# A planned attention and gated-MLP kernel: copies as 64-bit additions on GpSimd, more exponentials on VectorE, and a new order of work

## The chip, the cores and the metric

The kernel runs on one core of one Trainium2 chip. The core has five engines with an instruction queue each: TensorE (PE, matrix multiplication into the accumulation memory PSUM), VectorE (DVE), ScalarE (ACT, functions such as the exponential), GpSimd (POOL) and SyncE (SP, which here only issues transfers). The metric is the time of one execution on the device in microseconds (us); the median of several runs is given.

## What is computed

All tensors are bfloat16. Attention A and a gated MLP B read the same tokens x (B's own input is not used), and a gate per token mixes them:

```python
S, D, H, F = 2048, 512, 32, 1376           # Dh = D // H = 16
q, k, v = split(x @ wqkv)                   # 32 heads of 16
p = softmax(einsum("hqd,hkd->hqk", q, k) * Dh ** -0.5)
a = merge(einsum("hqk,hkd->hqd", p, v)) @ wo
b = ((x @ w_gate) * (x @ w_up)) @ w_down
g = sigmoid((x * gate_w).sum(-1, keepdims=True))
return g * a + (1 - g) * b
```

The exponentials of the scores, 32 x 2048 x 2048 of them, are most of the work outside PE.

## The kernel before

**A plan written by the program.** Nothing here is scheduled on the chip. When the program is built, the class `_Sched` plays the five engines forward in time with a table of durations. At every step each free engine takes a job by rules that read parameters from `PAR`; most of these are lists of (count, value), one value for each slot of 4 us of planned time (`g`). Each job taken becomes an instruction at the end of its engine's queue, and `_Plan.emit` adds the semaphore waits that its inputs and its reused buffers need. So the lists in `PAR` set the order of the work, and each engine then runs its queue strictly in that order.

**PE in halves.** Nearly all matmuls use half of the array's rows (64) and a quarter of its columns (32 or 17). `pe64` (line 1620) issues four of them, one for each column tile: a unit. The plan keeps two streams of units, r = 0 and r = 1, for the two halves of the rows.

**Scores.** Queries are taken in 32 groups ("quads") of four heads by 512 queries, keys in 16 tiles of 128: 512 key steps. A key step has four cells; a cell is one unit of score matmuls into one PSUM bank, 128 keys x 512 queries for one head. Seven of the eight banks are shared by the cells and the other results (`bank_pick`, `bank_put`); the eighth collects the weighted values.

**Two ways to the exponential.** A key step is of kind A or D.
- Kind A goes to ACT (`try_act`, `exp`, line 1718). One instruction takes one bank, or two adjacent ones.
- Kind D goes to DVE (`dve_pass`, `dpass`, line 1754): a scaled score plus a constant, cut at zero and written as a 16-bit integer, is the bit pattern of a bfloat16 that approximates the exponential. To make it accurate, four variants are summed: the pattern itself (v = 0) and three copies with 32 v added to each 16-bit integer (`copy`), each multiplied by values scaled by 2^(−v/4) (`Vs`, line 1777). A copy covers a whole key step, 128 x 2048 integers ("full"), or half of one. It is made on DVE (`copy_dve`, line 1760) or on POOL (`try_pool`, line 1764), where it is a 32-bit addition of two tensors, the pattern and the broadcast constant `cadd`. `dlst` holds the six key tiles that may be of kind D (`dks`), and `dl` caps how many of them a quad takes. Patterns lie in the buffers `DB` and, late in the run, in the space of `wv` and `wk`.

**Values.** `v_job` multiplies the cells by V with a column of ones: 8 matmuls for a key step of kind A, 4 x 8 for one of kind D. After 16 key steps DVE empties the bank (`o_copy`, line 1830); the denominators go by SP's transfers through DRAM and come back as the broadcast tile `rb`, and POOL multiplies (`mult`, line 1923, as a `ptask` of the plan).

**Fill units.** Between these run the projections, the MLP and the output matmuls (`fill`), a list of units in the order of their due times; each is emptied by DVE. `xt` units turn a tile of x by a multiplication with the identity `ident`, in 32 x 64 pieces in this kernel.

**DVE against POOL.** The plan keeps POOL's work and DVE's copies apart in time (`dve4_until`, `lock_v`), and each POOL copy and `mult` waits for the last DVE copy planned before it (`last4`).

**The beginning.** `prologue` loads x and the first weights, makes `ident` on POOL (line 1947), clears `QM`, turns the first 512 tokens and projects the first heads.

Of the kernel before, what the change touches and what calls it, by code (L numbers as in the profile page):

```python
# [10 lines left out]
I32 = mybir.dt.int32  # L11
# [121 lines left out]
class _Step:  # L133
    __slots__ = ("q", "kt", "kind", "cells", "nexp", "eops", "nv", "vleft", "buf", "npass", "ncp", "cpb", "okt", "cptodo", "ydone", "refs", "half", "acc")


class _Sched:
# [39 lines left out]
    def g(self, name):  # L177
        v = self.tab[name]
        return v[min(int(self.now / 4.0), len(v) - 1)]
# [38 lines left out]
    def next_d(self):  # L218
        while self.qd < self.NG:
# [7 lines left out]
            if self.dlst[m] and self.nd[m] < lim:  # L227
# [16 lines left out]
                e.acc = self.nd[m] <= self.g("acc")  # L244
                if e.acc:
                    e.cpb[3] = e.buf
                    e.cptodo = e.cptodo[:4]
# [17 lines left out]
    def bank_pick(self, kind, r):  # L265
# [15 lines left out]
        if kind == "D" and self.g("dpair"):  # L281
            a = self.dmate
            if a is not None and a[0] != r:
                self.dmate = None
                if a[1] in fr:
                    return a[1]
            d = 1 - 2 * r
            for b in fr:
                if b + d in fr and (b - d not in fr or self.g("dpair") > 1):
                    self.dmate = (r, b + d)  # L290
                    return b
# [71 lines left out]
    def v_job(self, r):  # L363
# [16 lines left out]
        if self.owner == 1 - r and self.g("hold") > 0 and not self.g("ph"):  # L380
            o = sum(1 for x in self.vq[1 - r] if x[0] <= self.now + 1e-9 and x[1].q == oq)
            if o and n < o + self.g("hold"):
                return False
# [122 lines left out]
    def y_unref(self, e, op):  # L506
        e.refs += 1
        e.eops.append(op)
        if e.acc and e.refs == 5:
            self.accq.append((e, list(e.eops), self.now + self.par["adel"]))  # L510
            self.at(self.now + self.par["adel"])
        elif e.refs == 7:
            self.dlast[e.buf] = list(e.eops)
            self.dfree.append(e.buf)
# [84 lines left out]
    def f_start(self, r):  # L599
# [13 lines left out]
        u.bank = self.bank_get("F")  # L613
        u.half = r
        self.fact.append(u)
        self.f_slice(u, r)
        return True

# [7 lines left out]
    def try_pe(self, r):  # L626
        if self.hf[r] > self.now + 1e-9:
            return False
        if self.g("ph"):
            if self.pe_phase(r):  # L630
                return True
            if r == 0 and self.par["t0"] <= self.now < self.par["warmto"] and self.owner is None and self.oq == 0:
                if self.hw:
                    self.o_evop = self.hw.warm_mm(r)
                self.log("pe%d" % r, 0.216, ("W", r))
                self.take(r, 0.216)
                return True
            return False
        if self.aout < self.g("alook") and self.s_a(r):
            return True  # L640
        if self.dout < self.g("dlook") and self.s_d(r):
            return True
        prog = (sum(self.apos) + sum(self.dpos)) / 64.0
        debt = self.target(prog) - self.fdone
        prio = self.g("prio") if debt <= self.g("fdebt") else self.g("prio2")
        for ch in prio:
            if ch == "A":
                if self.s_a(r):
                    return True
            elif ch == "D":  # L650
                if self.dout < self.g("dlook2") and self.s_d(r):
                    return True
            elif ch == "V":
                if self.v_job(r):
                    return True
            elif ch == "C":
                if self.f_cont(r):
                    return True
            elif ch == "S":
                if debt >= -self.g("flead") and self.f_start(r):  # L660
                    return True
        return False

    def pe_phase(self, r):
        self.tick[0] += 1
        o = self.ov[0].get(self.tick[0], 0)
        if o == 6:
            return False
        if o and (self.s_a, self.s_d, self.v_job, self.f_cont, self.f_start)[o - 1](r):
            return True  # L670
# [48 lines left out]

    def try_act(self):  # L720
# [15 lines left out]
        self.tick[2] += 1  # L736
        o = self.ov[2].get(self.tick[2], 0)
# [10 lines left out]
        if grp is not None and self.cfree[grp]:  # L748
            n = 1
            if len(self.cfree[grp]) > 1:  # L750
                for i in range(len(rd)):
                    j = next((j for j in range(i + 1, len(rd)) if abs(rd[j][4] - rd[i][4]) == 1), None)
                    if j is not None and (i == 0 or self.g("apick")):
                        x, y = rd[i], rd[j]
                        rd.remove(x)
                        rd.remove(y)
                        rd[:0] = [x, y]
                        n = 2
                        break
                if n == 1 and o == 2:  # L760
                    n = 0
                if n == 1 and o != 1 and any(abs(x[4] - rd[0][4]) == 1 and x[0] <= self.now + self.g("await") for x in self.aready):
# [6 lines left out]
        cells = [self.cfree[grp].pop(0) for _ in range(n)]  # L769
        cells.sort()  # L770
        rd.sort(key=lambda x: x[4])
        dur = 0.833e-3 * 512 * n + 0.051
# [10 lines left out]
        t = self.now + dur + 0.12 + 0.05  # L783
# [20 lines left out]
    def try_dve(self):  # L804
# [3 lines left out]
        self.tick[1] += 1  # L808
        o = self.ov[1].get(self.tick[1], 0)
        if o == 4:  # L810
            return False
        if o == 1 and self.lock_v <= now and self.copy_dve():
            return True
        if o == 2 and self.dve_pass(now):
            return True
        if o == 3 and self.dve_evac(now):
            return True
# [1418 lines left out]
```

## Time and profile before

| | |
|---|---|
| three runs, median (lowest to highest) | 714.14 us (712.85 to 715.62) |
| span of the profiled execution | 713.9 us |
| granted TensorE clock, mean | 0.995 |
| matmuls | 22279 |
| DVE, ACT, POOL instructions | 1095, 888, 426 |

Times in the views are microseconds unless marked ns. A row of a group names line, engine and operation, output <- input by the program's names, the shapes and the count, then the busy time in total and the mean of one instruction, then the idle time before them and what ended it. PEld is PE's weight load, which overlaps matmuls. The end of a matmul is modelled, and successive instructions of an engine overlap in the records, so that the mean of one instruction is longer than the distance from its start to the next one's start.

### The profile page before, as it was taken

Reading aid. Unit: us, or ns where it says so; the run is one execution under the profiler, and the core shown is the slowest. Engines: PE = TensorE matmul, PEld = TensorE weight load, DVE = VectorE, ACT = ScalarE, POOL = GpSimd, SP = SyncE. Lnnn points to the kernel's source line nnn. Section 1 sums busy time; section 2 is a strip of 40 time slices with the busy share of each in tenths; the row PEclk is TensorE's granted clock in tenths of the full one; section 3 lists DMA queues with packets and bytes.
Section 4 is the critical chain, followed back from the end, with each engine's and each line's share of the span. In section 5 each row is a group of like instructions: output and inputs, shape, how many; then the busy total and the mean of one; then the engine's idle time right before and its main releaser. Section 6 shows DMA issues by size and latency. Waiting matters only on the chain.

```text
span 713.9 us, 48146 instructions
## 1 busy us (share of the span) xinstructions
PE 697.6 (98%) x22279; PEld 370.7 (52%) x22279; DVE 659.7 (92%) x1095; ACT 686.5 (96%) x888; POOL 443.4 (62%) x426
## 2 busy tenths in 40 slices
PE   7999999999999999999999999999999999999997
PEld 4555455555544545555554455545454555555453
DVE  4898999999999999999999999999999999999994
ACT  5799999999999999999999999999999999999995
POOL 3374686786655555666675666777675647777631
PEclk8999999999999999999999999999999999999999
DMA  9101422103010100100001010100001010010100
GB/s 189 35 5 31 113 66 57 13 4 108 12 41 5 35 20 15 32 12 28 12 18 29 13 34 20 35 12 14 26 6 42 11 40 16 12 28 17 31 19 33
DMA packets 32121, 22.98 MB, mean 32 GB/s; under 512 B 17356, under 2 KB 28524, under 8 KB 31920
## 3 DMA queue, kind: packets, MB, share of 16 engines
q1 hardware_dynamic: 30784, 18.86, 10.7%
q8 instruction: 174, 2.85, 1.7%
q0 software_dynamic: 176, 0.53, 0.3%
q10 hardware_dynamic: 960, 0.52, 0.3%
q14 instruction: 27, 0.22, 0.1%
HBM read 12.23 MB, written 2.36 MB: 20 GB/s over the span
## 4 chain that ended last, share of the span: by engine, by line
PE 84%; DVE 7%; ACT 5%; issue 2%; DMA 1%; POOL 0%; SPq 0%; ACTq 0%; DVEq 0%
PE ps L1620 84%; DVE DB L1754 3%; ACT PT L1718 2%; ACT xT L1718 1%; DVE DB L1760 1%; DMA wg<-in_B_w_gate_dram 1%; DMA DB<-in_A_x_dram 1%; ACT wd L1718 1%; ACT hT L1718 0%; DVE wk L1754 0%; DVE oc L1830 0%; DVE wv L1760 0%; DVE hT L1806 0%; DVE oraw L1830 0%; ACT wu L1718 0%
## 5 line engine op out<-in xcount | busy, mean ns | idle before, releaser
L1620 PE MATMUL ps<-QM,KT 64*32 64x512 bf16 x8192 | 515.6, 380 | 4.6 <-ACT PT L1718 1.4
L1718 ACT ACTIVATE PT<-ps 128x1024 bf16<-128x1024 f32 (+1 forms) x453 | 384.7, 972 | 4.4 <-PE ps L1620 3.4
L1764 POOL TENSOR_TENSOR DB<-DB,cadd 128x512 int32<-128x512 int32 (+1 forms) x249 | 264.0, 1085 | 141.0 <-DVE DB L1760 88.4
L1754 DVE TENSOR_SCALAR DB<-ps 128x512 int16<-128x512 f32 x501 | 330.2, 687 | 22.6 <-PE ps L1620 18.6
L1620 PE MATMUL ps<-DB,Vs 64*17 64x512 bf16 x2912 | 267.7, 376 | 1.4 <-issue 0.3
L1620 PEld LDWEIGHTS ps<-QM,KT 64*32 64x32 bf16 x8192 | 161.1, 90 | 169.4 <-ACT PT L1718 49.0
L1718 ACT ACTIVATE xT<-ps 128x1024 bf16<-128x1024 f32 (+1 forms) x279 | 237.1, 951 | 1.7 <-PE ps L1620 1.3
L1620 PE MATMUL ps<-PT,Vp 64*17 64x512 bf16 x1556 | 219.4, 376 | 0.2
L1620 PE MATMUL ps<-xT,Vp 64*17 64x512 bf16 x936 | 151.9, 377 | 0.5 <-DVE oraw L1830 0.4
L1620 PE MATMUL ps<-xT,wu 64*32 64x512 bf16 x1376 | 113.7, 377 | 0.0
L1620 PE MATMUL ps<-xT,wg 64*32 64x512 bf16 x1376 | 113.0, 377 | 0.5 <-issue 0.4
L1760 DVE TENSOR_SCALAR DB<-DB 128x2048 int16<-128x2048 int16 (+1 forms) x170 | 109.8, 676 | 1.6 <-PE ps L1620 1.3
L1620 PE MATMUL ps<-DB,Vp 64*17 64x512 bf16 x1008 | 99.9, 377 | 0.7 <-DVE oc L1830 0.2
L1620 PE MATMUL ps<-wd,hT 64*32 64x512 bf16 x1408 | 100.2, 377 | 0.0
L1620 PEld LDWEIGHTS ps<-DB,Vs 64*17 64x17 bf16 x2912 | 73.4, 86 | 34.5 <-PE ps L1620 9.2
L1620 PEld LDWEIGHTS ps<-PT,Vp 64*17 64x17 bf16 x1556 | 55.5, 86 | 16.6 <-PE ps L1620 5.7
L1718 ACT ACTIVATE wd<-ps 128x1024 bf16<-128x1024 f32 (+1 forms) x74 | 61.4, 948 | 0.3 <-PE ps L1620 0.2
L1764 POOL TENSOR_TENSOR wv<-DB,cadd 128x512 int32<-128x512 int32 (+1 forms) x41 | 44.6, 1102 | 22.2 <-DVE DB L1760 12.7
L1764 POOL TENSOR_TENSOR wk<-DB,cadd 128x512 int32<-128x512 int32 (+1 forms) x33 | 35.5, 1092 | 21.0 <-DVE DB L1760 10.7
L1764 POOL TENSOR_TENSOR DB<-wk,cadd 128x512 int32<-128x512 int32 (+1 forms) x32 | 35.0, 1120 | 16.4 <-DVE DB L1760 12.4
L1620 PEld LDWEIGHTS ps<-xT,wu 64*32 64x32 bf16 x1376 | 36.3, 91 | 15.5 <-DVE DB L1754 2.5
L1620 PEld LDWEIGHTS ps<-xT,Vp 64*17 64x17 bf16 x936 | 38.2, 87 | 11.7 <-PE ps L1620 1.4
(111 smaller groups left out, 890.9 us busy)
## 6 DMA issues: line engine op xcount, KB each, us to landing
rb<-rscr SPq DMA_DIRECT2D x16, 256.0 KB
QM<-qraw SPq DMA_DIRECT2D x124, 16.0 KB, 2.2
oc<-oraw SPq DMA_DIRECT2D x60, 32.0 KB, 2.3
out_dram<-ost SPq DMA_DIRECT2D x12, 128.0 KB, 1.8
wd<-in_B_w_down_dram SPq DMA_DIRECT2D x10, 128.0 KB, 2.5
wu<-in_B_w_up_dram SPq DMA_DIRECT2D x12, 96.0 KB, 3.3
wg<-in_B_w_gate_dram SPq DMA_DIRECT2D x12, 96.0 KB, 2.2
OT<-in_A_x_dram SPq DMA_DIRECT2D x2, 256.0 KB, 4.6
```

What stands on the lines that cost most here:

```text
L1620: o = pe.matmul(dst, lhs, rhs, start=st, stop=sp, tile_position=(64 * r, 32 * cc), skip_group_check=True)
L1718: return self.P.op("act", lambda a: a.activation(dst, src, ACT.Exp, scale=self.ES), deps)
L1754: return self.dve(lambda v: v.tensor_scalar(dst, src, self.YB, 0.0, ALU.add, ALU.max), deps)
L1760: return self.dve(lambda e: e.tensor_scalar(o, a, 32.0 * v, None, ALU.add), deps)
L1764: lambda e: e.tensor_tensor(o.bitcast(I32), a.bitcast(I32), self.cadd[:, v, :].bitcast(I32).to_broadcast([128, n]), ALU.add),
```

## The change

The result stays the same formula; who does what, and when, changes.
- **Copies on POOL** become one 64-bit integer addition with a constant in the instruction: 32 v in each of the four 16-bit lanes. `cadd` goes. The planned durations are 1.026 (full) and 0.595 (half) in place of 1.849 and 0.997. A dummy addition in the prologue calls the operation once.
- **More kind D**: the lists give 178 of 512 key steps to DVE's way (150 before).
- **`mult`** moves from POOL to DVE, and so does one addition of the tail.
- **Exponentials** may take three banks of equal spacing (`tri`, `evenly`). **Evictions of kind D** may pair any two cells whose banks are adjacent, of two key steps too.
- **`xt` units** become four full-array matmuls that occupy both halves (`x_full`, `x_turn`).
- **The identity** is made on DVE: a counter along the row, its transpose, and a comparison.
- **`q_mask`** waits for the clearing of its own half of `QM` only.
- Branches that were switched off (`acc`, `ov`, `warm_mm`, another PE policy) are deleted.
- **All lists of `PAR` are new.** They come from a beam search over the plan. They change the order on every engine, and how many copies DVE makes.

Instructions in the two built programs, where they differ in number:

| | before | after |
|---|---|---|
| ACT exponentials of one, two, three banks | 302, 573, 0 | 719, 307, 1 |
| DVE evictions of kind D, one and two banks | 592, 4 | 700, 6 |
| DVE copies, full and half | 233, 21 | 27, 1 |
| POOL copies, full and half | 21, 371 | 410, 193 |
| `mult` on POOL, on DVE | 16, 0 | 0, 16 |
| weighted-value matmuls | 7696 | 8368 |
| matmuls that turn x in `xt` units | 128 | 16 |

```diff
     def copy(self, eng, src, dst, v, hs, deps):
...
-            lambda e: e.tensor_tensor(o.bitcast(I32), a.bitcast(I32), self.cadd[:, v, :].bitcast(I32).to_broadcast([128, n]), ALU.add),
-            deps + [self.r["cadd"]],
+        return self.P.op("pool", lambda e: e.int64_add(o.bitcast(I64), a.bitcast(I64), 32 * v * 0x0001000100010001), deps)
...
             if both and bl >= self.g("gfull"):
-                hs, dur = [0, 1], 1.849
+                hs, dur = [0, 1], 1.026
             elif bl >= self.g("ghalf"):
-                hs, dur = [h], 0.997
+                hs, dur = [h], 0.595
...
     def mult(self, bi, deps):
-        return self.P.op("pool", lambda g: g.tensor_tensor(self.OT[:, bi % 8, :], self.oc[:], self.rb[:], ALU.mult), deps)
+        return self.dve(lambda v: v.tensor_tensor(self.OT[:, bi % 8, :], self.oc[:], self.rb[:], ALU.mult), deps)
...
+    def x_turn(self, bank, ch, t, deps):
...
+            for kt in range(4):
+                c0 = 128 * kt
+                o = pe.matmul(self.ps[:, bank, c0 : c0 + 128], x[:, c0 : c0 + 128], self.ident[:], start=True, stop=True, skip_group_check=True)
...
     def exp(self, banks, cells, deps):
-        if len(banks) == 2:
-            s = cells[1][1] - i
-            dst = t[:, i : cells[1][1] + 1 : s, :]
-            src = self.ps[:, banks[0] : banks[1] + 1, :]
+        if len(banks) > 1:
+            dst = t[:, i : cells[-1][1] + 1 : cells[1][1] - i, :]
+            src = self.ps[:, banks[0] : banks[-1] + 1, :]
...
     def dve_pass(self, now):
-                if y[2] is x[2] and abs(y[4] - x[4]) == 1 and (y[4] - x[4]) * (y[3] - x[3]) > 0:
+                if abs(y[4] - x[4]) == 1 and (y[2] is x[2] or max(x[2].buf, y[2].buf) < self.par["ND"]):
...
+    def identity(self):
+        a, b = self.io[:, 0, :], self.io[:, 1, :]
...
+        for k in range(5):
+            w = a.rearrange("p (x y z) -> p x y z", y=2, z=1 << k)[:, :, 1, :]
+            o = dve(lambda v, w=w, k=k: v.tensor_scalar(w, w, float(1 << k), None, ALU.add), [o])
+        o = dve(lambda v: v.transpose(b, a), [o])
+            r.append(dve(lambda v, lo=lo, hi=hi: v.tensor_tensor(self.ident[lo:hi, lo:hi], self.io[lo:hi, 0, :], self.io[lo:hi, 1, :], ALU.is_equal), [o, z]))
...
-        i0 = pool(lambda g: g.memset(self.ident[:], 1.0))
-        i1 = pool(lambda g: g.affine_select(self.ident[:], self.ident[:], [[-1, 128]], ALU.is_equal, 0.0, base=0, channel_multiplier=1), [i0])
+        i1 = self.identity()
...
+        l0 = pool(lambda g: g.memset(self.lib[:], 0.0))
+        pool(lambda g: g.int64_add(self.lib[:].bitcast(I64), self.lib[:].bitcast(I64), 0), [l0])
...
- 'dl': ((2, 6), (1, 4), (4, 3), (1, 4), (3, 2), (4, 3), (2, 4), (3, 5), (3, 4), (3, 5), (6, 6), (4, 5),
+ 'dl': ((7, 6), (1, 5), (2, 6), (4, 5), (19, 6), (1, 3), (5, 6), (2, 5), (17, 6), (3, 5), (5, 7), (15, 6), (2, 7), (1, 6), (4, 7), (8, 6), (1, 7),
...
```

439 lines of the change are left out of this document (184 added, 255 removed), and 37 rows, old and new, of the table PAR.

## The prediction

> **What bounds the kernel now.** I read the page first: its span, the busy time of the engines and the shares of the chain that ended last.
>
> ```profile
> span 713.9 us, 48146 instructions
> PE 697.6 (98%) x22279; PEld 370.7 (52%) x22279; DVE 659.7 (92%) x1095; ACT 686.5 (96%) x888; POOL 443.4 (62%) x426
> PE 84%; DVE 7%; ACT 5%; issue 2%; DMA 1%; POOL 0%; SPq 0%; ACTq 0%; DVEq 0%
> ```
>
> One number looks decisive and is not: the 98% of PE (TensorE). A matmul row lasts about 376 ns while its successor starts earlier, and the chain gives PE 84% because some matmul is always under way. So I take a price per unit of work for each engine from the timeline, where a group and the next one show the start-to-start spacing, and multiply by counts. ScalarE (ACT) first: six two-bank exponentials and the row after them, then four one-bank ones and the row after them.
>
> ```profile
> 303.21 5.64 ACT L1718 ACTIVATE PT<-ps 128x1024 bf16<-128x1024 f32 x6
> 308.64 2.04 ACT L1718 ACTIVATE xT<-ps 128x1024 bf16<-128x1024 f32 x2
> 21.50 2.06 ACT L1718 ACTIVATE wg<-ps 128x512 bf16<-128x512 f32 x4 [4.35 <-PE ps L1620]
> 23.43 2.21 ACT L1718 ACTIVATE wu<-ps 128x512 bf16<-128x512 f32 x4
> ```
>
> (308.64 − 303.21) / 6 = 0.905 us for a pair, (23.43 − 21.50) / 4 = 0.4825 us for a single: 0.4225 us for each cell and 0.06 us for each instruction. A cell is one bank, 128 keys by 512 queries; there are 2048. VectorE (DVE) and PE in the same view:
>
> ```profile
> 310.81 1.87 DVE L1754 TENSOR_SCALAR DB<-ps 128x512 int16<-128x512 f32 x3
> 312.61 0.68 DVE L1760 TENSOR_SCALAR DB<-DB 128x2048 int16<-128x2048 int16 x1
> 313.21 0.68 DVE L1760 TENSOR_SCALAR wk<-DB 128x2048 int16<-128x2048 int16 x1
> ...
> 438.77 0.10 PEld L1620 LDWEIGHTS ps<-wd,hT 64*32 64x32 bf16 x4
> 438.81 0.10 PEld L1620 LDWEIGHTS ps<-PT,Vp 64*17 64x17 bf16 x4
> 438.99 0.10 PEld L1620 LDWEIGHTS ps<-QM,KT 64*32 64x32 bf16 x4
> 439.02 0.10 PEld L1620 LDWEIGHTS ps<-DB,Vs 64*17 64x17 bf16 x4
> ```
>
> A one-bank DVE eviction costs (312.61 − 310.81) / 3 = 0.60 us, and a full DVE copy (four cells) 313.21 − 312.61 = 0.60 us as well. On PE two streams of weight loads interleave, one for each half of the array; in each a unit of four matmuls follows the last after 0.21 to 0.22 us. I take 0.216 us for half the array, so 0.108 us of PE for a unit.
>
> Counts are from the two built programs' instruction lists. Before: 596 evictions (592 singles, 4 pairs) take 600 cells, so ACT has 1448 cells in 875 exponentials, 573 pairs and 302 singles.
> - ACT: 573 x 0.905 + 302 x 0.4825 + about 6 for the rest = 670 us.
> - PE: 5532 units x 0.108 = 597 us, and 2 us of transposes.
> - DVE: 592 x 0.60 + 4 x 1.13 + 233 full copies x 0.60 + 21 half copies x 0.335 = 506 us, and some 130 us of other evictions and small work: about 636 us.
> - GpSimd (POOL): 443 us busy by the page.
>
> How full the engines are by stretch (busy us, then counts in brackets):
>
> ```profile
> 0.00:20.00 20.00, 16.25 (x319) 9.69 (x327) 9.72 (x22) 10.08 (x17) 7.60 (x17) 0.85 0.96 189
> 20.00:100.00 80.00, 79.03 (x2588) 43.21 (x2580) 72.82 (x130) 76.51 (x116) 47.97 (x45) 1.00 0.17 41
> 300.00:400.00 100.00, 99.13 (x3160) 52.26 (x3151) 95.77 (x158) 99.45 (x111) 63.91 (x63) 1.00 0.07 18
> 400.00:500.00 100.00, 99.37 (x3296) 51.92 (x3288) 94.68 (x155) 99.88 (x125) 70.57 (x71) 1.00 0.08 22
> 700.00:714.00 14.00, 9.42 (x286) 4.31 (x269) 5.19 (x12) 5.59 (x9) 2.24 (x2) 0.98 0.12 41
> sum 714.00, PE 697.61 PEld 370.69 DVE 659.70 ACT 686.49 POOL 443.36; mean PE 69.76 PEld 37.07 DVE 65.97 ACT 68.65 POOL 44.34
> ```
>
> From 300 to 500 ACT is idle for 0.67 of 200 us; DVE lacks 9.6 us. PE's 3296 matmuls from 400 to 500 are 824 units, 89 of 100 us. ACT is the engine whose work lies nearest the span: ACT bounds the middle, with PE and DVE close behind. The 44 us between 713.9 and 670 I split: idle at the ends 9.9 (0 to 20) + 3.5 (20 to 100) + 8.4 (700 to 714) = 21.8; other idle 27.5 − 21.8 = 5.7; and 686.5 − 670 = 16.5 inside "busy" rows that lasted longer than their work. So 22 us of waiting lie inside the run. Who waits for whom:
>
> ```profile
> PEld ps L1620 <- ACT PT L1718: 50.4, 197, 0.9
> PEld ps L1620 <- ACT xT L1718: 28.1, 109, 0.6
> PEld ps L1620 <- DVE DB L1754: 27.5, 120, 1.5
> POOL DB L1764 <- DVE DB L1760: 115.4, 59, 10.0
> ```
>
> PE's weight loads wait for ACT and DVE to give banks back (50.4, 28.1, 27.5 us), and POOL stands 115.4 us behind DVE's copies.
>
> **The change, part by part.** First, *112 cells move from ACT to DVE* (178 key steps instead of 150: 712 cells). After the change ACT has 1336 cells in 1027 exponentials: 719 singles, 307 pairs, one triple. ACT: 719 x 0.4825 + 307 x 0.905 + 1.3 + 6 = 632 us, 38 less; 47 saved by the cells, 9 given back by 152 more instructions. The triple has no row; between a pair (0.905) and three singles (1.45) it is one instruction, so the choice is worth nothing.
>
> Second, *the copies go to POOL*. These rows give the prices (mean ns of one in the last column but one):
>
> ```profile
> L1754 DVE TENSOR_SCALAR DB<-ps 128x512 int16<-128x512 f32 x498 | 326.8, 684 | 21.9 <-PE ps L1620 18.0
> L1754 DVE TENSOR_SCALAR DB<-ps 128x1024 int16<-128x1024 f32 x3 | 3.7, 1222 | 0.7 <-PE ps L1620 0.7
> L1760 DVE TENSOR_SCALAR DB<-DB 128x2048 int16<-128x2048 int16 x160 | 106.5, 692 | 1.6 <-PE ps L1620 1.3
> L1760 DVE TENSOR_SCALAR DB<-DB 128x1024 int16<-128x1024 int16 x10 | 4.2, 418 | 0.0
> L1764 POOL TENSOR_TENSOR DB<-DB,cadd 128x512 int32<-128x512 int32 x236 | 239.9, 1040 | 133.0 <-DVE DB L1760 82.2 <-PE ps L1620 33.7 <-DVE wk L1760 6.9
> L1764 POOL TENSOR_TENSOR DB<-DB,cadd 128x1024 int32<-128x1024 int32 x13 | 24.5, 1893 | 8.1 <-DVE DB L1760 6.1 <-PE ps L1620 2.0
> L1923 POOL TENSOR_TENSOR OT<-oc,rb 128x512 bf16<-128x512 f32 x16 | 20.5, 1281 | 33.0 <-DVE DB L1760 26.0 <-DVE wv L1760 5.4 <-DVE wk L1760 1.6
> L1956 POOL MEMSET Vp<- 128x1024 bf16 x1 | 1.0, 1013 | 0.0
> L1957 POOL MEMSET erow<- 128x512 f32 x1 | 0.5, 529 | 0.0
> ```
>
> DVE loses 206 full copies (−123.6) and 20 half ones (418 ns, of which I count 0.335 as in the 0.08 us overlap of the others: −6.7). It gains 108 single evictions (+64.8), two pairs (+2.3 at 1.13, the 1222 ns row less overlap) and 16 multiplications of 128x512 (+9.6). Sum −53.6: about 582 us.
>
> POOL gets 410 full and 193 half copies as 64-bit additions with one tensor input. No row shows that operation. From above: the 32-bit additions with two inputs, 1893 and 1040 ns for the same bytes (1.67 ns per 32-bit word). From below: 64-bit elements each at the memset's step, (1013 − 529) / 512 = 0.945 ns, 512 elements, about 0.53 for a full copy. Nearest I think is the memset at one 32-bit word per step: one stream, 1013 ns full and 529 ns half. That value gives 410 x 1.013 + 193 x 0.529 = 517 us; the upper bound 410 x 1.893 + 193 x 1.040 = 977 us. Only the second end touches the forecast (rival 1).
>
> [...] No run here yet shows the one-input form.
>
> Third, *what the move adds to PE*. A key step on DVE needs 4 variants x 8 value matmuls instead of 8: 28 x 24 = 672 matmuls, 168 units, +18.1 us. PE: 597 + 18 + 2 = 617 us. The transposes of x shrink from 128 small matmuls to 16 full ones that take both halves; both forms are near 2 us in the first 20 us, where the engines wait for data: nothing.
>
> Fourth, *the rest*. The identity on DVE is a dozen tiny operations ahead of the first transposes; DVE stands idle there until 4.93 us. [...]
>
> ```profile
> 4.93 0.69 DVE L2009 CAST xT<-ps 128x512 bf16<-128x512 f32 x1 [3.27 <-PE ps L2002]
> 18.93 2.04 POOL L1764 TENSOR_TENSOR DB<-DB,cadd 128x512 int32<-128x512 int32 x2 [9.96 <-DVE DB L1760]
> ```
>
> [...] The 16 multiplications now wait on DVE for a broadcast DMA, and evictions queue behind them, for whose banks PE waits: 0 to 1 us each, 0 to 16 us; I take 0 and keep 16 for the range, since between the DMA and the use the plan keeps the same margin as before. The new order of work takes no work away; it can only shift the 22 us of waiting.
>
> **The sum.** ACT stays the longest: 632, against PE 617, DVE 582, POOL 517. Add the ends, 21.8, since no edit shortens the loads or the tail: 654. Then the inner waiting, 22 us before. Less: 206 copies of 0.60 us no longer stand ahead of evictions on DVE, and POOL's 115 us behind them go. More: PE would fill 617 of some 640 us instead of 599 of 692 us, so a lost slot is harder to win back. Bounds: none (654) to nearly double (694). I take a third, 7 us: 632 + 22 + 7 = 661 us. The trace's span of 713.9 us is the median of 714.14 us to 0.03%, so nothing is added around it: 661 us.
>
> **The rivals.**
> 1. *POOL's price.* If the 64-bit addition costs what the 32-bit ones did, POOL needs 977 us, and with its first copy at 18.9 us the run ends near 1000 us: slower. It decides from the price at which POOL reaches about 625 us (661 less its start and the tail): with a half at 0.52 of a full, 625 / (410 + 193 x 0.52) = 1.22 us for a full copy; at 1.33 us the time is back at 714. For it: the bytes and the engine are the same. Against: the memset rows, and one input instead of two.
> 2. *PE's slots are the bound already.* If PE cannot fill more than the 599 / 713.9 = 84% of now, 617 / 0.84 = 735 us: slower. For it: the chain is 84% PE, and weight loads wait for banks. Against: 89% in the stretch 400 to 500, and ACT busy for 99.7% of 300 to 500. [...]
> 3. *Singles starve ACT.* Here eight singles took (444.74 − 439.58) / 8 = 0.645 us each:
>
> ```profile
> 439.58 5.37 ACT L1718 ACTIVATE PT<-ps 128x512 bf16<-128x512 f32 x8
> 444.74 1.61 ACT L1718 ACTIVATE xT<-ps 128x1024 bf16<-128x1024 f32 x2
> ```
>
>    Twice as many singles may mean more of this. If the waiting inside the run grows with their number, 22 x 719 / 302 = 52 us in place of 7: 632 + 22 + 52 = 706; half of that growth gives 691 us. Against: the four singles above ran at 0.4825.
> 4. *The ends shrink too.* ACT is idle for 13.4 us before 100 us; if the new order halves that and the inner waiting vanishes, 632 + 15 = 647 us.
>
> **How the numbers follow.** Forecast 58%, rival 4 15%, rival 3 18%, rival 1 5%, rival 2 4%. The range 644 to 694 takes in rival 4 and the cheaper half of rival 3, and leaves out the two slow rivals and rival 3's worst. About 0.5% (3.6 us) is what this measurement can tell from no change. Faster: 58 + 15 + 18 = 91%; within 0.5%: 1%, from prices of POOL between; slower: 8%.
>
> **What would show it right or wrong.** POOL: full copies near 1.0 us start to start, 500 to 550 us busy; above 1.2 us the forecast falls. ACT: about 1040 instructions and 632 us of work, over 98% busy in the middle. DVE: near 590 us busy, with few copy rows. PE: 5700 units in some 640 us are 890 in 100 us of the middle (7120 matmuls in 200 us); if it stays near 824 while ACT shows gaps, rival 2 holds. If ACT's singles average well over 0.60 us and PE's weight loads wait more than 106 us on banks, rival 3. A multiplication on DVE with an idle stretch before it would show the added wait.

## The result, and the profile after

The changed kernel takes 702.29 us in the median of 4 runs (699.92 to 705.51), beside 713.65 us before: ratio 0.9844 (95% interval 0.9812 to 0.9877). It is faster, by 1.6%, where 7.4% were forecast, and outside the range of 644 to 694 us. The profiled execution has a span of 703.7 us and its own time of 705.51 us. The same kernel was measured twice more, on other chips, as the base of experiments. One run of after_again and two of after_third are over 1.5% slower than the fastest beside them; without these the medians are 686.9 and 688.9 us.

| chip | before, median | changed, median (lowest to highest) | ratio (95%) | fetch of a program packet, median |
|---|---|---|---|---|
| first | 713.65 | 702.29 (699.92 to 705.51) | 0.9844 (0.9812 to 0.9877) | 1.10 us |
| of after_again | 710.70 | 687.29 (680.95 to 692.84) | 0.9640 (0.9593 to 0.9687) | 0.96 us |
| of after_third | 711.39 | 690.58 (684.22 to 696.21) | 0.9732 (0.9694 to 0.9770) | 0.96 us |

The kernel before moves by 3 us from chip to chip, the changed one by 15, and by up to 12 on one chip. On the two later chips the time lies inside the forecast range, but 26 and 30 us above the 661 that were forecast. The last column is how long one transfer of TensorE's instruction queue (q8 in the page), a packet of 16.4 KB of its program, took in the profiled execution; it is read from the trace's transfer records.

The page of the changed kernel, first chip: span, busy times, that queue (packets, MB, share of 16 engines' span), and the chain that ended last:

```profile
span 703.7 us, 49393 instructions
PE 682.0 (97%) x22839; PEld 393.0 (56%) x22839; DVE 624.5 (89%) x1008; ACT 660.0 (94%) x1040; POOL 545.3 (77%) x617
...
q8 instruction: 178, 2.92, 1.8%
...
PE 92%; DVE 4%; issue 2%; POOL 1%; ACT 0%; DVEq 0%; POOLq 0%; ACTq 0%
```

POOL's 545 us and ACT's 1040 instructions are what was forecast. DVE is busy for 624.5 us where near 590 were foretold. ACT is busy for 94% only, and the chain is PE for 92% (84% before). By stretch; the columns are the stretch, its length, the busy us and counts of PE, PEld, DVE, ACT and POOL, then the granted clock, the share of the transfer engines and GB/s:

```profile
200.00:300.00 100.00, 99.24 (x3408) 58.62 (x3402) 87.95 (x138) 98.07 (x160) 89.96 (x110) 1.00 0.10 26
300.00:400.00 100.00, 96.29 (x3264) 53.22 (x3256) 92.57 (x141) 94.17 (x143) 85.70 (x90) 0.98 0.07 18
400.00:500.00 100.00, 97.17 (x3340) 56.24 (x3320) 88.72 (x141) 94.88 (x158) 80.37 (x94) 1.00 0.09 25
```

The first of these stretches in the kernel before (the prediction shows the other two):

```profile
200.00:300.00 100.00, 98.80 (x3033) 49.92 (x3025) 96.79 (x161) 98.37 (x124) 54.29 (x51) 1.00 0.09 25
```

PE does 3264 to 3408 matmuls in 100 us, 816 to 852 units, where 890 were forecast and where 758 to 824 stood before; ACT, at 98.4, 99.4 and 99.9% in these stretches before, is now at 98.1, 94.2 and 94.9%. Who waits for whom (us in total, times, longest):

```profile
PEld ps L1574 <- DVE DB L1710: 41.8, 177, 0.9
PEld ps L1574 <- issue: 36.7, 88, 1.5
PEld ps L1574 <- ACT PT L1671: 11.5, 52, 0.5
PEld ps L1574 <- ACT xT L1671: 8.4, 36, 0.6
PEld ps L1574 <- DVE wk L1710: 8.2, 17, 4.1
```

The waits for ACT's tiles PT and xT went from 78.5 us (50.4 + 28.1) to 19.9: ACT holds PE up far less. The line that grew most is "issue", 36.7 us, time in which a weight load waited for nothing that the profile shows. The same line before the change:

```profile
PEld ps L1620 <- issue: 15.4, 38, 2.3
```

The chain of the changed kernel, piece by piece (start, length, what), shows where these stops lie:

```profile
99.80 3.84 PE ps L1574 x127
103.64 0.59 issue
104.23 3.85 PE ps L1574 x128
```

The chain runs through 127 or 128 matmuls, 3.84 us, stops for 0.59 us and runs through the next 128. With their weight loads 128 matmuls are 256 instructions; a packet of program is 2.92 MB / 178 = 16.4 KB, 64 bytes each for 256; and 178 packets of 256 are 45568, close to twice the 22839 matmuls. That q8 is TensorE's is read from such counts: it has 174 packets for the 22279 matmuls before, 143 for 18375 in merge_fill, and 63 for 8192 in m256, where PE works nearly alone. So PE pauses where a packet ends, as far as the spacing tells; m256 below shows it without anything else in the way. The prediction has no term for this.

### The profile page after: what moved, and what is told of

Read it like the earlier page. It is cut to its first block, busy times and chain, and to the rows that moved or that the text cites. A ratio compares the mean times of both kernels' runs of the same rounds, so it can differ in the third digit from the quotient of the medians.

```text
span 703.7 us, 49393 instructions
## 1 busy us (share of the span) xinstructions
PE 682.0 (97%) x22839; PEld 393.0 (56%) x22839; DVE 624.5 (89%) x1008; ACT 660.0 (94%) x1040; POOL 545.3 (77%) x617
## 3 DMA queue, kind: packets, MB, share of 16 engines
q1 hardware_dynamic: 30784, 18.86, 10.6%
q8 instruction: 178, 2.92, 1.8%
## 4 chain that ended last, share of the span: by engine, by line
PE 92%; DVE 4%; issue 2%; POOL 1%; ACT 0%; DVEq 0%; POOLq 0%; ACTq 0%
PE ps L1574 92%; DVE DB L1710 1%; DVE OT L1869 1%; POOL DB L1717 1%; PE ps L1978 0%; DVE io L1880 0%; ACT wu L1671 0%; PE ps L1963 0%; DVE hT L1848 0%; ACT wd L1671 0%; POOL wk L1717 0%; DVE wk L1710 0%; DVE gden L1697 0%; DVE ident L1885 0%; DVE qraw L1732 0%
## 5 line engine op out<-in xcount | busy, mean ns | idle before, releaser
L1574 PE MATMUL ps<-QM,KT 64*32 64x512 bf16 x8192 | 560.1, 379 | 6.9 <-DVE wk L1710 3.6
L1717 POOL INT64_ADD DB<-DB x402 | 362.5, 917 | 94.8 <-PE ps L1574 36.4
L1710 DVE TENSOR_SCALAR DB<-ps 128x512 int16<-128x512 f32 x595 | 391.4, 690 | 42.2 <-PE ps L1574 38.0
L1671 ACT ACTIVATE PT<-ps 128x512 bf16<-128x512 f32 (+1 forms) x574 | 376.8, 749 | 11.4 <-PE ps L1574 10.3
L1574 PE MATMUL ps<-DB,Vs 64*17 64x512 bf16 x3448 | 320.3, 377 | 2.6 <-issue 1.8
L1671 ACT ACTIVATE xT<-ps 128x512 bf16<-128x512 f32 (+1 forms) x288 | 205.5, 779 | 10.3 <-PE ps L1574 8.8
L1671 ACT ACTIVATE wd<-ps 128x512 bf16<-128x512 f32 (+1 forms) x101 | 66.1, 740 | 3.4 <-PE ps L1574 2.8
L1717 POOL INT64_ADD wv<-DB x65 | 56.1, 869 | 14.1 <-PE ps L1574 8.5
L1574 PE MATMUL ps<-wv,Vs 64*17 64x512 bf16 x472 | 48.8, 376 | 0.0
L1717 POOL INT64_ADD DB<-wk x46 | 42.4, 936 | 7.5 <-DVE wk L1710 6.8
```

The costliest lines, as they stand in the source:

```text
L1574: o = pe.matmul(dst, lhs, rhs, start=st, stop=sp, tile_position=(64 * r, 32 * cc), skip_group_check=True)
L1671: return self.P.op("act", lambda a: a.activation(dst, src, ACT.Exp, scale=self.ES), deps)
L1710: return self.dve(lambda v: v.tensor_scalar(dst, src, self.YB, 0.0, ALU.add, ALU.max), deps)
L1717: return self.P.op("pool", lambda e: e.int64_add(o.bitcast(I64), a.bitcast(I64), 32 * v * 0x0001000100010001), deps)
```

## The experiments

Where an addition below "costs" so much, it is set against the changed kernel on a chip with like fetches. The theories that the expectations name: A, TensorE's program comes in too slowly; B, the multiplications that are now on VectorE (and their waits); C, ScalarE still sets the pace; D, PE loses time at each change of the tile's shape; E and F are stated where they appear.

**m512 and m256: PE alone.** A kernel of 2048 units without weights or banks to wait for, nothing else of the reference; once with 512 columns for each matmul, once with 256. One run of each.

```diff
-COLS = 512
+COLS = 256
```

> TensorE alone: 2048 units of four 64x32 matmuls of 512 columns, alternating between the two halves of the rows, with no wait inside; everything else of the kernel is left out and the output is not the reference's. At 0.108 us a unit this is 221 us. Theory A (TensorE's instruction supply pauses once per packet of 16 KB, that is once per 128 weight loads and 128 matmuls, by 0.3 to 0.5 us, and the new plan has no slack to hide it): 64 packets cost 19 to 32 us more, 240 to 253 us from the first to the last matmul, with one gap per 128 weight loads. Rival B (the borders cost nothing; the loss comes from the new waits on VectorE): 221 us, no regular gap.

> The same stream with 256 columns per matmul, so half the work and the same number of instructions. Theory A as a fixed pause per packet: 111 + 64 x 0.3 to 0.5 = 130 to 143 us. Theory A as a lowest period of a packet (the smallest distance of two packets in the changed kernel is 3.3 us): 64 x 3.3 = 211 us. Rival B: 111 us.

Measured: 245.28 and 248.22 us. These include the start and the output's transfers; from the first matmul to the last it is 231.1 and 227.3 us. So the 240 to 253 us that A gave for m512 are missed, A having put the pause per packet too high, and for m256 so are the 211 of A's lowest period. But half the columns take as long. In the view by stretches, 200 us of m512 and then of m256:

```profile
20.00:220.00 200.00, 197.61 (x7183) 114.90 (x7168) 0.00 (x0) 0.00 (x0) 0.00 (x0) 1.00 0.02 5
```

```profile
20.00:220.00 200.00, 110.02 (x7168) 97.92 (x7168) 0.00 (x0) 0.00 (x0) 0.00 (x0) 0.99 0.02 5
```

Both do 7168 weight loads in 200 us, 56 packets, 3.57 us each, though PE is busy for 197.6 us in one and 110.0 us in the other. The timeline of m256 shows what fills the rest:

```profile
42.14 1.94 PE L40 MATMUL ps<-x,w 64*32 64x256 bf16 x128 [1.51 <-issue]
45.60 1.94 PE L40 MATMUL ps<-x,w 64*32 64x256 bf16 x128 [1.51 <-issue]
49.05 1.94 PE L40 MATMUL ps<-x,w 64*32 64x256 bf16 x128 [1.51 <-issue]
52.50 1.94 PE L40 MATMUL ps<-x,w 64*32 64x256 bf16 x128 [1.51 <-issue]
56.23 1.94 PE L40 MATMUL ps<-x,w 64*32 64x256 bf16 x128 [1.79 <-issue]
```

128 matmuls run in 1.94 us, then PE stands until the next 128 start, 3.45 us after the last, sometimes 3.73: the pace is that of the packets, not of the matmuls and not of single instructions. Of the 62 distances in the trace 40 are 3.45 us, 18 about 3.73 and 4 are 4.00, 3.57 in the mean. At that mean 178 packets need 178 x 3.57 = 636 us. A holds as a period of the packets, not as a fixed pause.

The trace also shows what goes with the longer distances: the fetch that began last before a packet started, some 2.4 us earlier. Where that fetch took up to 1.05 us (42 packets) the distance is 3.49 us in the mean; from 1.05 to 1.25 us (12) 3.64; above 1.25 us (8) 3.87, and none of these 8 is at 3.45.

**add_pe: more units.**

```diff
+        self.many += 1
+        if self.many % 11 == 0:
+            mms += mms
         return self.pe64(r, mms, deps)
```

> The changed kernel with every eleventh unit of score matmuls issued twice (186 units, 744 matmuls, 20 us of TensorE work, 6 more packets). Theory A (TensorE sets the pace in nearly all of the run): the 20 us and 6 pauses come through nearly whole, 718 to 725 us. Rival C (ScalarE still sets the pace, as the prediction had it): less than half, 702 to 711 us.

Measured: 708.40 us, ratio 0.9966 (0.9946 to 0.9986), with fetches of 0.96 us. Against 687.29 and 690.58 us for the changed kernel at such fetches that is 18 to 21 us for six more packets (6 x 3.57 = 21.4); against the 702 us that the expectation started from it looked like 6. Added work on PE is paid nearly in full, as far as bases from other chips can tell. Whether it is paid as program or as columns needs pv256.

**pv256: fewer columns, as many instructions.** Part of the value sums is left out.

```diff
-            mms.append((self.ps[32 * cc : 32 * cc + 17, 7, :], w, self.cell(cells[cc], lo, hi), first, True, cc))
+            n = 512 if first else 256
+            mms.append((self.ps[32 * cc : 32 * cc + 17, 7, 0:n], w, self.cell(cells[cc], lo, hi)[:, 0:n], first, True, cc))
```

> The changed kernel with every value matmul after the first of its accumulation cut from 512 columns to 256 (part of the value sums is left out): as many instructions and packets, but some 2,060 units with half the array time, 2,060 x 0.054 = 111 us less. A: the program still needs 178 x 3.57 = 636 us, with 22 us at the ends 658, and no more than the stalls above that go: 658 to 695, mean distance of packets 3.5 to 3.8, and TensorE's waits put down to issue grow well beyond 36.7 us. Rival (array time sets the pace): ScalarE is next, 632 + 22 = 654 us, TensorE's added waits are for ScalarE and VectorE, and those for issue stay at or below 37 us.

Measured: 688.99 us, ratio 0.9696 (0.9644 to 0.9748), fetches 0.96 us: within 2 us of the changed kernel, though by the expectation's estimate the array has 111 us less to do. The columns alone did not set the pace. PE's waits in this run:

```profile
PEld ps L1574 <- ACT PT L1672: 38.7, 150, 0.6
PEld ps L1574 <- issue: 28.8, 63, 1.8
PEld ps L1574 <- ACT xT L1672: 22.5, 83, 0.7
```

The time is inside A's 658 to 695 us, but A's sign is missed: the waits for "issue" did not grow beyond 36.7 us, only beyond the 18.5 of the changed kernel at like fetches (after_again below). Those for ACT's PT and xT grew from 26.3 there to 61.2 us, which was the rival's sign. With the columns gone ACT is close behind, which pv256_act below prices.

**add_nop: meant as more instructions without work.**

```diff
+        self.many += 1
+        quiet = self.many % 4 == 0
...
+            if quiet:
+                pe.nop(nofuse=True)
```

> The changed kernel with one empty TensorE instruction after every fourth unit: some 1,425 instructions more, no matmul and no column more; 1,425 / 256 is about 5.6 packets of program. A (TensorE's program supply, 3.57 us a packet by m256): 5.6 x 3.57 = 20 us at most; since six further packets full of work cost 8.6 us in add_pe, 5 to 20 us more than the changed kernel's 702: 707 to 722. Rival (array time sets the pace; a no-op takes none): 700 to 704, and add_pe's 8.6 us were its 744 matmuls.

Measured: 735.13 us, ratio 1.0338 (1.0294 to 1.0382), with fetches of 0.96 us. The program grew by 689 instructions, not 1425 (181 packets). The supply would charge 689 / 256 x 3.57 = 9.6 us; the run pays 45 to 48 us, 65 to 70 ns for each. The line of the empty instruction, and PE's waits:

```profile
L1578 PEldq EVENT_SEMAPHORE  x701: 51/51/51, 9.2 to 731.4; - x176
```

```profile
PEld ps L1580 <- issue: 115.6, 285, 2.1
```

Neither expectation is met, and the edit did something else than was meant. What the trace has at that line are 701 semaphore waits of 51 ns each; weight loads that carry a wait fell by as many, from 2789 to 2088. So the empty instruction took over the wait of the unit behind it, and no other one is left. The run shows that a wait as an instruction of its own costs PE more than the bytes of its program; it tells nothing for or against A.

**merge_fill and merge_all: fewer instructions.** Fill units as one matmul of 64 x 128 in place of four of 64 x 32; in merge_all the scores too.

```diff
+            mms = [(self.ps[:, bank, :], w, x, start, stop, -1)]
```

> The changed kernel, same plan and order; in the fill units (projections, MLP, outputs) the four matmuls of 64x32, whose weights lie side by side and whose moving data is the same, become one of 64x128. 4608 of 22841 matmuls are left out of TensorE's program (three in four of 6144), which then has about 142 packets in place of 178; the work is the same. Theory A (the supply of TensorE's program, 3.57 us per packet, is what the plan does not know and what holds the order back): the pauses fall by a fifth or more and the time comes towards the planned order, 675 to 692 us. Rival D (a change between 64x32 and 64x128 makes the array run empty): each of the thousands of changes costs 0.1 to 0.4 us, 800 us or more.

> As merge_fill, and the four 64x32 matmuls of a score unit become one of 64x128 too (6144 fewer): about 12100 matmuls, 94 packets, so that the supply has more than half its time to spare. Only the value matmuls stay at 64x17. Theory A without a price for the change of shape: no pause at borders is left, and what remains is the plan with its other slips, 662 to 680 us. Rival D: slower still than merge_fill, as scores and values alternate everywhere.

Measured: 1462.22 us, ratio 2.0524 (2.0483 to 2.0565), and 2241 to 2324 us, at granted clocks of 0.80 and 0.56 to 0.59. Of the first, its busy time, program and longest wait:

```profile
PE 1451.8 (99%) x18375; PEld 391.1 (27%) x18375; DVE 647.7 (44%) x1008; ACT 718.9 (49%) x1040; POOL 545.7 (37%) x617
...
q8 instruction: 143, 2.34, 0.7%
```

```profile
PEld ps L1574 <- issue: 845.0, 2433, 0.8
```

The program shrinks to 143 packets, and the time doubles; if all of it scaled with the clock, 1462 x 0.80 = 1170 us would be left, still far above 702. The timeline shows D, a stop at each change between shapes:

```profile
703.64 0.39 PE L1574 MATMUL ps<-DB,Vs 64*17 64x512 bf16 x4
703.70 0.39 PE L1574 MATMUL ps<-QM,KT 64*32 64x512 bf16 x4
704.02 0.39 PE L1574 MATMUL ps<-wd,hT 64*128 64x512 bf16 x1
704.34 0.41 PE L1574 MATMUL ps<-QM,KT 64*32 64x512 bf16 x8
```

A matmul of 64 x 128 starts 0.32 us after the 64 x 32 before it, and the next 64 x 32 again 0.32 us later; two of 64 x 128 in a row are 0.11 us apart in the median (146 of them). The trace has 1342 changes each way, 0.39 us in the mean, 1036 us in all. So merge_fill shows that the price of these changes is large, with 4464 matmuls less; what PE does in a stop the trace does not show.

**mult_pool: the multiplications on POOL again.**

```diff
-        return self.dve(lambda v: v.tensor_tensor(self.OT[:, bi % 8, :], self.oc[:], self.rb[:], ALU.mult), deps)
+        return self.P.op("pool", lambda g: g.tensor_tensor(self.OT[:, bi % 8, :], self.oc[:], self.rb[:], ALU.mult), deps)
```

> The changed kernel, same plan and order, with the 16 multiplications by the reciprocal denominators issued on GpSimd again. Theory A: the order and the TensorE stream are the same, so little changes, 698 to 704 us. Rival B (the multiplication on VectorE, 1281 ns each in place of the planned 598, and its wait for the broadcast transfer, is what eats the gain): most of the 16 x 0.7 us and of the wait of about 4 us near 375 us comes back, 685 to 692 us.

Measured: 906.06 us, ratio 1.2748 (1.2707 to 1.2788), with fetches of 0.96 us: outside both expectations. POOL's timeline around one of the 16:

```profile
248.97 1.25 POOL L1869 TENSOR_TENSOR OT<-oc,rb 128x512 bf16<-128x512 f32 x1 [6.73 <-issue]
255.99 4.08 POOL L1717 INT64_ADD DB<-DB  x4 [5.77 <-issue]
```

Before the multiplication POOL is idle for 6.73 us and before the next 64-bit addition for 5.77 us, without a releaser. At the 16 it is 6.7 to 8.1 and 5.7 to 6.3 us, 206 us in all; with the 1.25 us of each multiplication that is 226, and the run is 215 to 219 us longer than the changed kernel at like fetches. POOL pays at each turn between the two operations, in both directions; what it does in these stops the trace does not show. So the multiplications had to go to DVE with the copies: that is one change, not two.

**before_i64: the new copies in the old order.** The order of before, with 64-bit additions on POOL (392 copies); the 16 multiplications and one addition of the tail on DVE, as in the changed kernel.

```diff
-            lambda e: e.tensor_tensor(o.bitcast(I32), a.bitcast(I32), self.cadd[:, v, :].bitcast(I32).to_broadcast([128, n]), ALU.add),
+        return self.P.op("pool", lambda e: e.int64_add(o.bitcast(mybir.dt.int64), a.bitcast(mybir.dt.int64), 32 * v * 0x0001000100010001), deps)
```

> [...] A: GpSimd was not the bound and TensorE has the same 174 packets: 708 to 718. Rival (cheaper copies are what made the changed kernel faster): 702 or below. Added VectorE work of 16 x 1.28 = 20 us, if VectorE bounds: 725 or above.

Measured: 721.65 us, ratio 1.0149 (1.0120 to 1.0179). POOL's busy time fell from 443.4 to 254.1 us, and nothing was gained. Of the 10.6 us lost on its chip (711.1 us before), 5.8 lie at the start, where the first loads of `ident` on PE come at 9.61 instead of 3.83 us. Before, and then in this run:

```profile
3.83 0.15 PEld L2002 LDWEIGHTS ps<-ident,DB 128*128 128x128 bf16 x1 [0.28 <-issue]
```

```profile
0.80 0.20 POOL L1942 MEMSET ident<- 128x128 bf16 x1 [0.29 <-POOLq L2219]
...
9.27 0.28 POOL L1943 TENSOR_SCALAR_AFFINE_SELECT ident<-ident 128x128 bf16<-128x128 bf16 x1 [8.26 <-issue]
...
9.61 1.62 PEld L2000 LDWEIGHTS ps<-ident,DB 128*128 128x128 bf16 x16 [6.06 <-POOL ident L1943]
```

POOL stands for 8.26 us, with no releaser, before the second step of the identity. That is what the identity on DVE avoids. The other 5 us fit 16 multiplications on a DVE that was 92% busy, but no run takes them alone. The new price of POOL's copies gives no time in the old order; that it buys the room to move cells from ACT fits this, but no run takes the move alone.

**before_act: was ScalarE the bound before?**

```diff
+        op = self.P.op("act", lambda e: e.activation(dst, src, ACT.Exp, scale=self.ES), deps)
+        self.many += 1
+        if self.many % 8 == 0:
+            op = self.P.op("act", lambda e: e.activation(dst, src, ACT.Exp, scale=self.ES), [op])
+        return op
```

> The kernel before with every eighth one-bank exponential made twice: 37 or so more, 37 x 0.48 = 18 us of ScalarE, as add_act did to the changed kernel, where it cost nothing. If ScalarE set the pace before, as the prediction's first part says, and TensorE's program does now: 10 to 18 us more than before, 722 to 732. Rival (TensorE's program, 174 x 3.57 = 621 us and its stalls, set the pace before as well): 0 to 5 us, 712 to 717.

Measured: 729.25 us, ratio 1.0266 (1.0250 to 1.0282), against 710.70 on its chip: 18.6 us for 18 us of work. ACT set the pace, to the full, as the prediction's first part says.

**add_act, add_dve, add_pool: the same question after.** Every eighteenth one-bank exponential twice (39 more, 19 us), every 22nd eviction (32, 19 us), every twentieth full POOL copy (20, 20.6 us), with the same few lines as in before_act.

> The changed kernel with every eighteenth one-bank exponential issued twice (39 more, about 19 us of ScalarE work, with a wait of about 0.1 us each for the first). Theory A (TensorE's supply sets most of the pace; adding 20 us of TensorE work cost 8.6 us): 2 to 8 us more, 704 to 710 us. Rival C (ScalarE sets the pace): 14 us or more, 716 us and up.

> The changed kernel with every 22nd eviction of a score bank issued twice (32 more, about 19 us of VectorE work, with a wait of about 0.1 us each for the first). Theory A: 0 to 6 us more, 702 to 708 us. Rival B (VectorE and what waits on it holds the order back): 12 us or more, 714 us and up.

> The changed kernel with every twentieth full copy on GpSimd made twice: 20 copies more, 20 x 1.03 = 20.6 us of GpSimd. A: 0 to 5 us, 701 to 707. Rival (copies that come late set the stalls): 10 us or more, 712 or above.

Measured: 699.60 us (ratio 0.9845, 0.9811 to 0.9879), 700.82 us (0.9856, 0.9817 to 0.9896) and 692.14 us (0.9738, 0.9705 to 0.9771), the first two on one chip; fetches 0.99, 1.05 and 0.96 us. Set against 702.29 us these additions cost nothing, and the third is a gain, which no theory had. So the base was in doubt, and was taken again beside them.

**after_again with add_pool_again, and after_third with add_act_again.** The kernels are unchanged; each pair ran on one chip.

> The changed kernel itself once more, beside add_pool_again on one chip. Rival E (how long a fetch of TensorE's program takes differs from chip to chip: median 1.10 us a packet in the profile of the changed kernel, 0.96 us in those of add_pool and pv256, and time goes with it): where fetches take 0.96 us the changed kernel takes 688 to 696 and add_pool's 692 is no gain; where they take 1.1 us both take 699 to 705. Rival F (later GpSimd copies really make the run shorter): 698 to 706 here and 688 to 696 for add_pool_again, whatever the fetches take.

> add_pool once more (every twentieth full GpSimd copy made twice), on the same chip as after_again. Rival E: within 4 us of after_again. Rival F: 6 to 12 us below it.

> The changed kernel a third time, as the base of add_act_again on one chip. By rival E of after_again (confirmed there: 687 us with fetches of 0.96 us in the median, 702 with 1.10): 683 to 692 if the fetches take 0.96 us, 698 to 705 if they take 1.1 us.

> add_act once more (39 one-bank exponentials made twice, 19 us of ScalarE), beside after_third, since add_act had been set against a changed kernel measured on another chip. A (TensorE's program supply sets the pace, ScalarE has slack): 0 to 5 us above after_third. C (ScalarE sets the pace where fetches are short): 12 to 19 us above it. Both engines together, as in pv256_act (7 us above pv256): 6 to 11 us.

Measured: after_again 687.29 and add_pool_again 691.24 us (0.9740, 0.9715 to 0.9764), fetches 0.96 us in both: E holds, and 20.6 us of POOL's work cost 4 us at most, which the spread of after_again (681 to 693) doesn't tell from nothing. The page and the waits of after_again stand against those of the first chip:

```profile
span 685.9 us, 49393 instructions
...
q8 instruction: 178, 2.92, 1.6%
```

```profile
PEld ps L1574 <- DVE DB L1710: 45.5, 196, 0.9
PEld ps L1574 <- issue: 18.5, 47, 2.1
PEld ps L1574 <- ACT PT L1671: 16.9, 78, 0.5
```

The same program with much the same waits, but for one: "issue" 18.5 us in place of 36.7. The difference, 18.2 us, is close to that of the spans, 703.7 − 685.9 = 17.8. The 178 fetches took 1.14 us each in the mean on the first chip and 1.02 us here. On the first chip 70 took up to 1.05 us, 50 up to 1.25 and 58 longer; here it is 128, 28 and 22. At the distances that m256 showed for these three kinds (3.49, 3.64 and 3.87 us) the program needs 651 us there and 634 us here, an estimate: 17 us apart, like the spans. No run sets the fetch time by hand, and why it differs is open.

after_third took 690.58 and add_act_again 698.15 us (0.9815, 0.9791 to 0.9840): 7.6 us for 19 us of ACT's work (9.3 from the 688.9), where the kernel before had paid 18.6 for 18. The expectation for two engines close together was 6 to 11. The runs of after_third spread over 12 us, so this tells some from none and from all, not how much. add_act had hidden it behind the base from another chip. For add_dve no base on its chip exists; it can't be told from add_act there (1.2 us), and what its 19 us of work cost is open.

**pv256_act: what holds pv256.** pv256 with the 39 exponentials of add_act.

> pv256 (value matmuls with 256 columns, part of the sums left out) with every eighteenth one-bank exponential made twice: 39 more, 19 us of ScalarE. A (the program's supply alone holds pv256 at 689): 0 to 5 us more, 687 to 694. Rival (with short value matmuls ScalarE is the bound again, and 689 us are its): 12 to 19 us more, 701 to 708.

Measured: 695.80 us, ratio 0.9792 (0.9777 to 0.9806): 6.8 us above pv256 (another chip, like fetches), between the two expectations and much as in the full kernel. With an estimated 111 us of columns less, ACT's 19 us are still paid by a third only.

## Why the prediction was right and wrong

**Right: what bounded the kernel, and which way it goes.** ACT set the pace before (before_act), 38 us of its work went, and the kernel became faster. ACT's price held: in the trace after, a one-bank exponential starts 0.477 us after a one-bank one in the median, and a two-bank one is followed after 0.92 us. That ACT would stay over 98% busy in the middle did not come true.

**Right: POOL.** 1.013 us had been taken for a full copy; five starts in a row below give 5.07 / 5 = 1.01 us, and POOL is busy for 545 us where 500 to 550 were foretold. Rival 1 falls.

**Off by 1 us: the identity at the start.** The five steps of its counter take 545 ns each in the mean:

```profile
1.25 2.86 DVE L1880 TENSOR_SCALAR io<-io 128x16 f32<-128x16 f32 x5
...
5.21 1.62 PEld L1963 LDWEIGHTS ps<-ident,DB 128*128 128x128 bf16 x16 [1.73 <-DVE ident L1885]
5.86 0.69 DVE L1970 CAST xT<-ps 128x512 bf16<-128x512 f32 x1 [0.18 <-PE ps L1963]
```

DVE's first CAST comes at 5.86 us instead of 4.93: 0.9 us, for which the sum has no term. POOL's first copy starts at 18.93 us, as before.

**Mis-sized: the multiplication on DVE.** 0.60 us was taken, and waiting was feared. The waiting is 1.7 us in all; the price is what was off:

```profile
L1869 DVE TENSOR_TENSOR OT<-oc,rb 128x512 bf16<-128x512 f32 x16 | 20.5, 1281 | 1.7 <-DMA rb<-rscr 1.7
```

1281 ns in the mean, 681 to 4919. POOL's and DVE's timelines around the longest:

```profile
371.50 5.08 POOL L1717 INT64_ADD DB<-DB  x5
376.57 1.03 POOL L1717 INT64_ADD wv<-DB  x1
```

```profile
373.23 4.92 DVE L1869 TENSOR_TENSOR OT<-oc,rb 128x512 bf16<-128x512 f32 x1
378.07 1.81 DVE L1710 TENSOR_SCALAR wk<-ps 128x1024 int16<-128x1024 f32 x2
```

The multiplication starts at 373.23 and ends 0.55 us after POOL's row of copies has ended at 377.60; four of these copies start after it, at 373.53 us and then 1.01 to 1.02 us apart. Of the 16, one that meets no copy takes 0.68 us, and those that start behind one copy 0.7 to 1.5. Why a copy beside it makes it longer the trace does not show. PE then waits for DVE's next eviction, 4.1 us in the longest wait for `wk`. after_again has such a case (4.95 us), after_third none. Beside the 9.6 us counted the row has 20.5: 11 us more of DVE's work. How much of it is in the time no run separates.

**Wrong: PE's term.** "PE: 597 + 18 + 2 = 617 us" takes 0.108 us for a unit from neighbours inside a packet, 3.46 us for 32 of them. That is the shortest distance of two packets in m256, not the mean. m512 and m256 give 3.57 us, 0.1116 us for a unit: 178 x 3.57 = 636 us, and by the estimate above 634 us with the fetches of after_again and 651 with those of the first chip. PE was thus the longest engine in the sum, ahead of ACT's 632, and its 890 units in 100 us would have needed 3.60 us for each packet, with hardly a loss.

**Wrong, and the larger part: the inner waiting.** "I take a third, 7 us: 632 + 22 + 7" supposed that ACT alone would set the pace. With 636 and the same ends, 21.8, the runs have 702 − 658 = 44 us of waiting on the first chip and 29 to 33 us on the two others; with 651 for the first chip's fetches it is 29 there too. A reading of this: where one engine leads, the others' stalls hide behind it; here two stand a few us apart, and a stall of either is not won back. add_act_again and pv256_act fit it: a third to a half of ACT's added work is paid, neither none nor all. That the whole waiting comes from this is argued, not shown.

**The rivals.** Rival 2, "PE's slots are the bound already", was nearest in mechanism: PE leads, and its sign, ACT with gaps while PE stays near 824 units in 100 us, came in two of the three stretches (816 and 835). It is not the array's time, as m256 and pv256 show, and its 735 us, from 84% of fill, were too many. PE's busy time told little: m512 and m256 keep one pace with 197.6 and 110.0 busy us of 200. PEld's 56% did not betray the limit either. Rival 3 (singles starve ACT) gave 691 us for half its growth, near the two later chips; its sign, over 106 us of PE's waits on banks, did not appear (41.8 + 11.5 + 8.4 = 61.7). A time that fits is no proof of a mechanism, and that these two chips fall inside the range is luck of the same kind. Rival 4 (smaller ends) cannot be told from the rest.

**Open.** How the 29 us and more of waiting that remain divide among packets, banks and DVE was not separated. At like fetches (after_again) PE's longest wait is for DVE to give banks back, 45.5 us where it was 27.5 before; what DVE's added work costs add_dve was to tell, and it has no base. No run set the fetch time, and none found a version faster than the changed kernel: fewer instructions for TensorE is where the runs point, but the one form tried costs the shape changes of merge_fill.

## What to carry to other kernels

Price an engine's unit over a long stretch of that engine alone, not from two neighbours: a period that repeats (here 256 instructions, 3.57 us) hides between them, and instructions, not columns, may be what an engine runs out of. When work is moved off the leading engine, look how far the next one is; here two came within a few per cent, and the waiting grew from 22 to 29 us and more where a third of it had been forecast. Look in the trace at what an added instruction became before reading its price. Measure the base again on the chip of the experiment before reading a few per cent from it.

## What was unexpected of the hardware

- In a stream of matmuls alone TensorE's program came in packets of 16.4 KB, 256 instructions by the counts, 3.45 us apart at the least and 3.57 us in the mean, and matmuls of 256 columns took as long as those of 512. Packets whose fetch took over 1.25 us were 3.87 us apart.
- One program differs by 15 us between chips (702.29 and 687.29), the profiled spans by 17.8 us, PE's waits for "issue" by 18.2.
- POOL stood for 6.7 to 8.1 us before a float multiplication and for 5.7 to 6.3 us before the next 64-bit addition, at each of 16 turns.
- A two-input multiplication on DVE took 4.92 us beside a row of POOL copies and ended 0.55 us after it, against 0.68 us with no copy beside it.
- A semaphore wait as an instruction of its own in TensorE's queue, in place of one on the weight load, cost 65 to 70 ns.
- A change between matmuls of 64 x 32 and 64 x 128 took 0.32 us from start to start, against 0.11 us for two of 64 x 128 in a row.
